# Seventh batch's one-hot rows on VectorE behind the last scores, gather tiles cleared later, its row units in other pairs, sixth batch's table as in the others

## The chip, the core and the metric

The kernel runs on one core of one Trainium2 chip. The time is device microseconds (us) of one execution; lower is better. TensorE is PE in the views (PEld its weight loads), VectorE is DVE, ScalarE is ACT, GpSimd is POOL, SyncE, which issues most transfers, is SP.

## The reference

Causal attention over 8 batches of 448 tokens (12 heads of 64) gives x (3584 x 768). A gate picks one of 8 experts for each token; each expert keeps the 80 tokens with the largest gate weights and sends them through two layers.

```python
scores = np.where(mask, -1000000000.0, scale * np.matmul(q, k.transpose(0, 1, 3, 2)))
attn = np.exp(scores - np.max(scores, axis=-1, keepdims=True))
x = np.matmul(attn / (np.sum(attn, axis=-1, keepdims=True) + 1e-09), v)   # then (N, D)
expert_idx = np.argmax(x @ w_gate, axis=1)        # gate_w: the softmax value there
for e in range(E):
    tok_idx = ...                                 # the 80 largest gate_w of expert e
    h = np.maximum(x[tok_idx] @ w1[e], 0.0)
    out[tok_idx] = gate_w[tok_idx, None] * (h @ w2[e])
```

## The kernel before

**Attention.** The program runs over 48 pairs of heads, six for each batch (batch 6 is b = 5, batch 7 b = 6, batch 8 b = 7). A pair has 8 slots. CYCLE says what stands in each: scores on PE in two parts (`s0`, `s1`, L354), the masked maximum on DVE (`m`, tile `ns`, L364), the exponential on ACT (`e`, tile `prob`, L371), the turn of the pair before in two halves on PE (`t0`, `t1`, tile `tp`, L385) with its copy on ACT (`c0`, `c1`, tile `PT`, L390), the product with v (`v`, tile `xp`, L411) and its copy on DVE (`xu`, L417). `tp` has a single buffer, so `t1` waits for the copy `c0`, and the next turn for `c1`.

**Selection.** The expert choice is a running table: every batch merges its tokens with a table of the best 80 of each expert so far. Its steps are spread over the pairs of the following batches, by tables of slot numbers that count from the end of the batch's own pairs: STEPS for most batches, NEXT for batch 6, EARLY for batch 7. What of batch 7 comes after the last pair (slot 48 on) is called in the order of TAIL, where `rest` takes the next such step, mixed with the whole selection of batch 8. The steps of importance here:

- `c3w` to `c0w`, `c3l` to `c0l`: weights compared on PE (tile `rn`), read out on DVE (`less`, L764); `rl`, `lt`: the same against the table (L782, L788); `cp`, `ro`: counts and places (L795, L800).
- `places`, `places_more`: one-hot rows `rm` of the table's entries. As a rule two DVE instructions of 80x320 (L820); where `late` is set, eight POOL instructions of 80x80 (L817).
- `gt`, `own`, `earlier`, `rank`: each token's rank; `own` is on DVE (L854, L856), `earlier` and `rank` on POOL (L849 to L859).
- `rr`: one-hot rows of the tokens (L883 on DVE, or with `late` four POOL instructions of 128x80, L879).
- `tn`: 8 products with `rm` (L893) and 4 with `rr` (L896) on PE make the new table; `tab` copies it (L907), `rp` turns it (L911), `row` copies that (L915).

**Rows of x.** They are turned on PE into two tiles `rt`, scaled into `xr` on DVE and stored to `xs` by SP: `row_tile` (L606, L617) for batches 1 to 6, `row_unit` (L576, L585) for batch 7. Its four units stand at the slots of ROWS_EARLY (head half, pair of token tiles, slot, distance of the second scaling). The tiles `rt`, `rn`, `rl`, `gp`, `tn`, `rp` and `selt` all come from `bank`, which up to the last pair has two buffers in turn (pool `ps_m`): the second tile asked for waits until the one two before it was read out.

**Batch 8** in the tail: gate products `gp` (L484), `gs` copied by ACT (L489), `lp` (L500), on DVE `lg`, `logit`, maximum, `gsh`, first pick `goh` (L512 to L661), the exponential `gex` on ACT (L648), `ggw` on DVE (L667), then the one-hot columns, their turns `selt` (L740) copied by ACT (L743), and the steps above. ACT also scales row group 2 (L547). `wp` (L1125) are products whose result nobody reads. `close` gives attention's memory free and clears the three tiles `xg` (L1113; one on DVE, two on POOL), into which the experts' rows are gathered later (L1214).

**Experts.** After batch 8's table the rows of each expert are gathered, weights are split into two halves `wh` (ACT, L1197) and `wl` (DVE, L1182), and freed weight buffers are loaded anew by SP (L200).

Of the kernel before, what the change touches and what calls it, by code (L numbers as in the profile page):

```python
# [28 lines left out]
NORMS = [0, 2, 3]  # L29
ROWS = [22, 30, 46, 54]  # L30
STEPS = {'c2w': 64, 'c1w': 72, 'cp': 72, 'gt': 80, 'tn': 88, 'rp': 92, 'row': 93, 'gp0': 16, 'gs0': 18, 'gp1': 24, 'gs1': 26, 'lp': 32, 'lg': 34, 'logit': 39, 'shifted': 40, 'chosen': 42, 'sums': 42, 'one_hot': 43, 'weight': 43, 'columns': 44, 'weighted': 44, 'parts': 45, 'r0t': 48, 'r1t': 48, 'r0c': 50, 'r1c': 50, 'c3w': 56, 'rl': 56, 'c0w': 56, 'c3l': 58, 'lt': 61, 'c0l': 63, 'c2l': 66, 'c1l': 74, 'ro': 74, 'places': 77, 'places_more': 77, 'own': 82, 'earlier': 83, 'rank': 83, 'rr': 85, 'rr_more': 85, 'tab': 90}
NEXT = {'c2w': 64, 'c1w': 72, 'cp': 72, 'gt': 80, 'tn': 86, 'rp': 88, 'row': 90, 'gp0': 16, 'gs0': 18, 'gp1': 24, 'gs1': 26, 'lp': 32, 'lg': 34, 'logit': 39, 'shifted': 40, 'chosen': 42, 'sums': 42, 'one_hot': 43, 'weight': 43, 'columns': 44, 'weighted': 44, 'parts': 45, 'r0t': 48, 'r1t': 48, 'r0c': 50, 'r1c': 50, 'c3w': 56, 'rl': 56, 'c0w': 56, 'c3l': 58, 'lt': 61, 'c0l': 58, 'c2l': 66, 'c1l': 74, 'ro': 74, 'places': 75, 'places_more': 75, 'own': 82, 'earlier': 83, 'rank': 83, 'rr': 83, 'rr_more': 83, 'tab': 87}
EARLY = {'gp0': 16, 'gs0': 18, 'gp1': 24, 'gs1': 26, 'lp': 32, 'lg': 34, 'logit': 35, 'shifted': 36, 'chosen': 38, 'sums': 38, 'one_hot': 39, 'weight': 39, 'weighted': 40, 'columns': 40, 'parts': 41, 'r0t': 45, 'r1t': 45, 'r0c': 46, 'r1c': 46, 'c3w': 48, 'rl': 49, 'c0w': 50, 'c3l': 51, 'c0l': 52, 'lt': 53, 'c2w': 54, 'c2l': 55, 'c1w': 56, 'c1l': 57, 'cp': 58, 'ro': 59, 'places': 60, 'places_more': 61, 'gt': 62, 'own': 63, 'earlier': 64, 'rank': 65, 'rr': 66, 'rr_more': 67, 'tn': 68, 'tab': 69, 'rp': 70, 'row': 71}
ROWS_EARLY = [(0, 0, 6, 1), (0, 1, 14, 1), (1, 0, 22, 4), (1, 1, 30, 4)]
LATE = 19

TAIL = """
rest3 ta ya v0 rest3 tb yb rest2 rest v1 rest2 turned vy guard invert placed rest w rest2 rest gp0 wy rest4 close piece gp1 gs
r0w r0e r1w lp rest r1e r1m rest rest r2w r2e r3w rest rest r3e lg logit shifted chosen r4w r4e r5w *2
sums one_hot wsum one_zero wmore columns r0t r0c *3 weight weighted parts hold rl r1t r1c *1 lt r3m r4m r5e r5m cp ro r6w r6e r6m  # L40
c3w c3l c2w r7w r7e r7m c2l c1w gt3 *2 c0w c1l gt2 *1 c0l *1 gt1 places *1 earlier gt0 places_more own *5 rank rr tn tab *28
"""
# [4 lines left out]
def attention_then_moe(  # L47
# [12 lines left out]
    nc = tc.nc  # L60
    B, _, NP, S = qT.shape
    N, D = out.shape
    E = wg.shape[2]
# [29 lines left out]
    def bank(shape, dtype, name):  # L93
        return (ps_x or ps_m).tile(shape, dtype, name=name, tag="x" if ps_x else "misc")
# [17 lines left out]
    NSL = (CAP + SL - 1) // SL  # L112
# [107 lines left out]
    lg = keep.tile([P, NT, H * E], F32, name="lg")  # L220
# [464 lines left out]
    def as_table(t):  # L685
        return t[:, 0:NV * E].rearrange("k (v e) -> k v e", e=E)
# [6 lines left out]
    def select_groups(bt):  # L693

        b = bt.b
        last = b == B - 1
        regular = b < B - 2 and CAP > 0
        late = b in (B - 3, B - 2)
        sm = lambda name, shape, dt=F32: spool.tile(shape, dt, name=name, tag=name, bufs=1)
        eng = nc.vector if last else nc.gpsimd  # L700

# [102 lines left out]
        def place(ro, sn, s, rm=None):  # L804

            n = min(SL, CAP - s * SL)
            halves = [(0, E // 2), (E // 2, E)]
            if rm is not None:
                halves.pop(0)
            elif NSL == 1:  # L810
                halves.pop()
            if rm is None:
                rm = spool.tile([SL, E, SL], BF16, name="rm", tag="rm", bufs=1 if NSL == 1 else 2)
            for e0, e1 in halves:
                if late:
                    for e in range(e0, e1):
                        nc.gpsimd.tensor_scalar(rm[0:sn, e, 0:n], slots_e[0:sn, s, e, 0:n], ro[0:sn, e:e + 1], None,  # L817
                                                op0=ALU.is_equal)
                    continue
                nc.vector.tensor_tensor(  # L820
                    out=rm[0:sn, e0:e1, 0:n], in0=ro[0:sn, e0:e1].unsqueeze(2).to_broadcast([sn, e1 - e0, n]),
                    in1=slots_e[0:sn, s, e0:e1, 0:n], op=ALU.is_equal)
            return rm
# [47 lines left out]
        def move(s):  # L871
            sn = min(SL, CAP - s * SL)
            got = {}

            def one_hot(t0=0, t1=NT):
                if t0 == 0:
                    got["rr"] = sm("rr", [P, NT, SL], BF16)
                for t in range(t0, t1) if late else []:
                    nc.gpsimd.tensor_scalar(got["rr"][:, t, 0:sn], slots_t[:, s, t, 0:sn], bt.rank[:, t:t + 1], None,  # L879
                                            op0=ALU.is_equal)  # L880
                if late:
                    return
                nc.vector.tensor_tensor(out=got["rr"][:, t0:t1, 0:sn],  # L883
                                        in0=bt.rank[:, t0:t1].unsqueeze(2).to_broadcast([P, t1 - t0, sn]),
                                        in1=slots_t[:, s, t0:t1, 0:sn], op=ALU.is_equal)

            def moved():
                m, moves, rr = bt.m, bt.moves, got["rr"]
                tn = got["tn"] = bank([SL, NV, E], F32, "tn")
                for i, (tab, ro, so) in enumerate(moves[:s + 1]):  # L890
                    rm = bt.places[i] if NSL == 1 else place(ro, so, s)
                    for e in range(E):
                        nc.tensor.matmul(tn[0:sn, :, e], rm[0:so, e, 0:sn], tab[0:so, :, e], start=(i == 0 and e == 0),  # L893
                                         stop=False, skip_group_check=True)
                for t in range(NT):
                    nc.tensor.matmul(tn[0:sn].rearrange("k v e -> k (v e)"), rr[:, t, 0:sn],  # L896
                                     m[:, t].rearrange("k v e -> k (v e)"), start=(t == 0 and not moves[:s + 1]),
                                     stop=(t == NT - 1), skip_group_check=True)

            def taken():  # L900
                tn, rr = got["tn"], got["rr"]
                if last:
                    finish(s, sn, tn)
                    return
                got["flat"] = tables[s][b % 2]
                tab = got["tab"] = as_table(got["flat"])
                (nc.scalar.copy if b >= B - 3 else nc.vector.tensor_copy)(tab[0:sn], tn[0:sn])  # L907

            def turn():
                rp = got["rp"] = bank([P, SL], BF16, "rp2")  # L910
                nc.tensor.transpose(rp[:, 0:sn], got["flat"][0:sn, 2 * E:2 * E + P], identb[0:sn, 0:sn])  # L911

            def row():
                row = table_rows[s][b % 2]
                (nc.scalar.copy if b >= B - 3 else nc.vector.tensor_copy)(row[0:3 * E, 0:sn], got["rp"][0:3 * E, 0:sn])  # L915
                bt.new.append((got["tab"], row))
                if s == NSL - 1:
                    table[:] = bt.new
            first, more = [one_hot], []
            if not last and NSL == 1:  # L920
                first, more = [lambda: one_hot(0, NT // 2)], [lambda: one_hot(NT // 2, NT)]
            bt.rest_of_rows = run(more)
            return first + [moved, taken] + ([] if last else [turn, row])
# [68 lines left out]
    def batch_plan(bt):  # L992
# [5 lines left out]
        if early:  # L998
            for g, half, at, x in ROWS_EARLY:
                for f, x in zip(row_unit(bt, g, half), (0, 1, x)):  # L1000
# [9 lines left out]
        if CAP:  # L1010
            steps.update(select_groups(bt))
        for name, at in (EARLY if early else NEXT if bt.b == B - 3 else STEPS).items():
            if name in steps:
# [3 lines left out]
    with tc.manual_schedule():  # L1017
# [18 lines left out]
        parts, values = [], []  # L1036
        for i, pr in enumerate(pairs):
# [22 lines left out]
            for k in range(SLOTS):  # L1060
# [9 lines left out]
                if i > 4 and k in (1, 4, 7):  # L1070
                    if not parts and len(wload) < WBUF:
                        parts = piece_parts()
# [10 lines left out]
        rest = [f for k in sorted(plan) for f in plan.pop(k)]  # L1083
# [10 lines left out]
        if CAP:  # L1094
            steps.update(select_groups(bt))
# [363 lines left out]
```

## Time and profile before

| | us |
|---|---|
| median of 3 runs | 449.97 (449.87 to 450.06) |
| the profiled execution | 450.27 |
| its span in the trace | 448.2 |
| PE, ACT, DVE, POOL busy | 421.9, 373.9, 344.8, 91.2 |
| mean granted clock of PE, share of full | 0.989 |

The profiled execution lies 0.30 us above the median, and 2.07 us of it lie outside the span. All times below are us from the start of the span. Attention's pairs end near 298, the tail with batch 8's selection runs to 326, the experts to the end.

### The profile page before, as it was taken

Reading aid. Unit: us, or ns where it says so; the run is one execution under the profiler, and the core shown is the slowest. Engines: PE = TensorE matmul, PEld = TensorE weight load, DVE = VectorE, ACT = ScalarE, POOL = GpSimd, SP = SyncE. Lnnn points to the kernel's source line nnn. Section 1 sums busy time; section 2 is a strip of 40 time slices with the busy share of each in tenths; the row PEclk is TensorE's granted clock in tenths of the full one; section 3 lists DMA queues with packets and bytes.
Section 4 is the critical chain, followed back from the end, with each engine's and each line's share of the span. In section 5 each row is a group of like instructions: output and inputs, shape, how many; then the busy total and the mean of one; then the engine's idle time right before and its main releaser. Section 6 shows DMA issues by size and latency. Waiting matters only on the chain.

```text
span 448.2 us, 18075 instructions
## 1 busy us (share of the span) xinstructions
PE 421.9 (94%) x7353; PEld 342.1 (76%) x7353; DVE 344.8 (77%) x1214; ACT 373.9 (83%) x982; POOL 91.2 (20%) x236
## 2 busy tenths in 40 slices
PE   5798999999999999999999999986998999999994
PEld 2566777777777777777777777864678999999993
DVE  4556578778978878788887887865577999999892
ACT  4999999989999898998998978872677889897891
POOL 4301002002102100300210210518440275211002
PEclk9999999999999999999999999999799999999998
DMA  8348589678884866767866352544359999999911
GB/s 307 114 148 305 186 300 318 191 279 290 258 296 173 289 238 247 252 198 272 287 208 223 116 197 89 205 145 158 106 171 341 405 400 389 392 424 424 397 40 44
DMA packets 33458, 110.07 MB, mean 246 GB/s; under 512 B 4274, under 2 KB 17074, under 8 KB 30176
## 3 DMA queue, kind: packets, MB, share of 16 engines
q1 hardware_dynamic: 32176, 105.19, 64.3%
q0 software_dynamic: 1056, 3.51, 2.5%
q8 instruction: 57, 0.93, 0.8%
q10 hardware_dynamic: 144, 0.23, 0.2%
q14 instruction: 25, 0.20, 0.1%
HBM read 85.35 MB, written 23.99 MB: 244 GB/s over the span
## 4 chain that ended last, share of the span: by engine, by line
PE 66%; ACT 16%; DVE 6%; issue 4%; DMA 4%; POOL 3%; POOLq 0%; DVEq 0%
PE sp L354 14%; PE xp L411 13%; ACT prob L371 10%; PE tp L385 9%; ACT PT L390 5%; PE op L1254 4%; PE op L1262 3%; PE hp L1269 3%; PE rt L606 3%; PE hp L1266 3%; PE hp L1268 3%; PE hp L1254 2%; DVE ns L364 2%; DMA xg<-xs,idx 2%; PE op L1264 2%
## 5 line engine op out<-in xcount | busy, mean ns | idle before, releaser
L371 ACT ACTIVATE prob<-ns,nb 128x448 f32<-128x448 f32 (+6 forms) x336 | 167.0, 500 | 26.8 <-DVE nb L364 26.5
L364 DVE CUSTOM_DVE_ANT_0 ns<-sp,mask 128x448 f32<-128x448 f32 (+6 forms) x336 | 124.0, 418 | 59.3 <-PE sp L354 35.1
L390 ACT COPY PT<-tp 128x1024 f32<-128x1024 f32 x96 | 95.9, 999 | 7.3 <-PE tp L385 7.0
L354 PE MATMUL sp<-qk 64*64 64x256 f32 (+6 forms) x1344 | 97.5, 396 | 4.5 <-DMA qk<-k_t 4.5
L411 PE MATMUL xp<-PT,vt 128*64 128x64 f32 (+3 forms) x1536 | 95.3, 277 | 0.0
L1182 DVE SCALAR_TENSOR_TENSOR wl<-wraw,wh 128x768 f16<-128x768 f32 (+1 forms) x91 | 91.8, 1065 | 3.0 <-ACT wh L1197 3.0
L411 PEld LDWEIGHTS xp<-PT,vt 128*64 128x64 f32 x1536 | 79.6, 137 | 17.6 <-issue 8.8
L1197 ACT ACTIVATE wh<-wraw 128x768 f16<-128x768 f32 (+1 forms) x91 | 78.9, 930 | 5.5 <-DMA xs<-xrl 1.7
L354 PEld LDWEIGHTS sp<-qk 64*64 64x64 f32 x1344 | 54.1, 134 | 35.8 <-issue 18.0
L385 PE MATMUL tp<-ident,prob 64*128 64x64 f32 x1536 | 68.0, 227 | 6.4 <-ACT PT L390 6.0
L385 PEld LDWEIGHTS tp<-ident,prob 64*128 64x128 f32 x1536 | 56.1, 139 | 17.0 <-ACT PT L390 8.7
L371 ACT ACTIVATION_READ_ACCUMULATOR prob<-ns,nb 128x1 f32 x336 | 63.7, 190 | 0.0
L1269 PEld LDWEIGHTS <-wl 128*128 128x128 f16 x362 | 36.1, 100 | 1.4 <-DVE wl L1182 1.4
L1268 PEld LDWEIGHTS <-wh 128*128 128x128 f16 x362 | 36.2, 100 | 0.6 <-issue 0.6
L1266 PEld LDWEIGHTS <-wh 128*128 128x128 f16 x362 | 36.4, 101 | 0.0
L417 DVE COPY xu<-xp 128x448 f32<-128x448 f32 x48 | 29.7, 619 | 8.4 <-PE xp L411 7.9
L1266 PE MATMUL hp<-xh,wh 128*128 128x80 f16 x320 | 35.3, 202 | 0.5 <-issue 0.5
L1269 PE MATMUL hp<-xh,wl 128*128 128x80 f16 x320 | 35.3, 202 | 0.0
L1268 PE MATMUL hp<-xl,wh 128*128 128x80 f16 x320 | 35.3, 202 | 0.0
L1355 POOL DMA_INDIRECT out<-yo,idx x8 | 19.7, 2466 | 65.1 <-ACT yo L1352 60.9
L1262 PE MATMUL op<-hh,wh 128*128 128x160 f16 x264 | 29.4, 233 | 0.0
L1264 PE MATMUL op<-hh,wl 128*128 128x80 f16 x264 | 28.9, 199 | 0.0
(185 smaller groups left out, 559.5 us busy)
## 6 DMA issues: line engine op xcount, KB each, us to landing
wraw<-w SPq DMA_DIRECT2D x25, 1536.0 KB, 11.2
out<-mask SPq DMA_DIRECT2D x56, 192.0 KB, 4.1
qk<-q_t SPq DMA_DIRECT2D x15, 672.0 KB, 5.1
qk<-k_t SPq DMA_DIRECT2D x15, 672.0 KB, 5.4
vt<-v_t SPq DMA_DIRECT2D x16, 576.0 KB, 7.5
wraw<-w SPq DMA_DIRECT2D x30, 256.0 KB, 5.0
xs<-xr SPq DMA_DIRECT2D x18, 384.0 KB, 4.5
wraw<-w SPq DMA_DIRECT2D x16, 192.0 KB, 4.5
```

What stands on the lines that cost most here:

```text
L354: nc.tensor.matmul(pr.sp[t][to], st["q"][rows, p, t * QB:(t + 1) * QB], st["k"][rows, p, 0:WIDTH[t]], start=True, stop=True)
L364: nc.vector.tensor_tensor_reduce(out=ns[:, 0:w], in0=pr.sp[t], in1=mask[:, S - w:S], scale=-1.0 / 8.0, scalar=HUGE, op0=ALU.add, op1=ALU.m ...
L371: nc.scalar.activation(pr.P[:, OFF[t]:OFF[t] + w], ns[:, 0:w], AF.Exp, bias=nb, scale=-1.0, accum_out=pr.sums[:, pr.p * TILES + t:pr.p * T ...
L385: nc.tensor.transpose(tp[:, r, at:at + QB], pr.P[rows, off:off + P], ident[rows, rows])
L390: (nc.scalar.copy if how == "a" else nc.vector.tensor_copy)(pr.PT[:, g], pr.tp)
L411: nc.tensor.matmul(xp[rows, x0 * QB:x1 * QB], st["vt"][:, c, p * P + j * DH:p * P + (j + 1) * DH], pr.PT[:, g, 1 - j if crossed else j, at ...
L1182: return nc.vector.scalar_tensor_tensor(out=l, in0=src, scalar=SW, in1=h, op0=ALU.mult, op1=ALU.subtract)
L1197: nc.scalar.activation(h, src, AF.Copy, scale=SW)
L1262: nc.tensor.matmul(side[i], wh[:, ws], u.both[:, c], start=(x == 0 and i % per == 0), stop=(x == n - 1), skip_group_check=True)
L1266: nc.tensor.matmul(o, wh[:, ws], ah[:, c, :], start=(x == 0 and i % per == 0), stop=False, skip_group_check=True)
L1268: nc.tensor.matmul(o, wh[:, ws], al[:, c, :], start=False, stop=False, skip_group_check=True)
L1269: nc.tensor.matmul(o, wl[:, ws], ah[:, c, :], start=False, stop=(x == n - 1), skip_group_check=True)
```

## The change

- `late` is set for batch 6 alone, so batch 7's `rm` and `rr` are DVE instructions (two of 80x320, and one of 128x320 instead of two half steps).
- `tab` and `row` run on ACT for batch 7 alone; batch 6's run on DVE.
- TAIL is in another order: `close` behind `rr` and `gp1`, `tn` ahead of `lp`, `ro` ahead of `placed`.
- ROWS_EARLY: the units stand at slots 14, 22, 30 and 46 instead of 6, 14, 22 and 30; the fourth one's second scaling falls in the tail.
- NEXT, batch 6: `tn` 86 to 88, `tab` 87 to 90, `rp` 88 to 92, `row` 90 to 93, `c3l` 58 to 61, `lt` 61 to 58, `places` 75 to 76.

```diff
-ROWS_EARLY = [(0, 0, 6, 1), (0, 1, 14, 1), (1, 0, 22, 4), (1, 1, 30, 4)]
+ROWS_EARLY = [(0, 0, 14, 1), (0, 1, 22, 4), (1, 0, 30, 4), (1, 1, 46, 8)]
...
-rest3 ta ya v0 rest3 tb yb rest2 rest v1 rest2 turned vy guard invert placed rest w rest2 rest gp0 wy rest4 close piece gp1 gs
-r0w r0e r1w lp rest r1e r1m rest rest r2w r2e r3w rest rest r3e lg logit shifted chosen r4w r4e r5w *2
+rest3 ta ya rest3 v0 tb yb rest3 rest v1 rest2 turned vy guard invert rest placed w rest2 rest gp0 wy rest5 gp1 close piece gs
+r0w r0e r1w rest lp r1e r1m rest rest r2w r2e r3w rest r3e lg logit shifted chosen r4w r4e r5w *2
...
-        late = b in (B - 3, B - 2)
+        late = b == B - 3
...
-                (nc.scalar.copy if b >= B - 3 else nc.vector.tensor_copy)(tab[0:sn], tn[0:sn])
+                (nc.scalar.copy if b == B - 2 else nc.vector.tensor_copy)(tab[0:sn], tn[0:sn])
...
-                (nc.scalar.copy if b >= B - 3 else nc.vector.tensor_copy)(row[0:3 * E, 0:sn], got["rp"][0:3 * E, 0:sn])
+                (nc.scalar.copy if b == B - 2 else nc.vector.tensor_copy)(row[0:3 * E, 0:sn], got["rp"][0:3 * E, 0:sn])
...
-            if not last and NSL == 1:
+            if b < B - 2 and NSL == 1:
                 first, more = [lambda: one_hot(0, NT // 2)], [lambda: one_hot(NT // 2, NT)]
```

On DVE in the tail, from batch 7's places to the first row group of batch 8 (`xrl`), - is before and + is now:

```order
 L431 RECIPROCAL sums<-sums 128x42
-L800 TENSOR_SCALAR rof_6693<-rn,pnum 80x8
+L800 TENSOR_SCALAR ro_6684<-rn,pnum 80x8
+L820 TENSOR_TENSOR rm<-ro_6684,slots_e 80x320 x2
 L417 COPY xu<-xp 128x448
 L854 TENSOR_TENSOR own<-gt,goh 128x32
 L856 TENSOR_REDUCE larger<-own 128x4
-L1113 MEMSET xg_6756 80x768
+L883 TENSOR_TENSOR rr<-rank,slots_t 128x320
+L1113 MEMSET xg_6752 80x768
 L553 TENSOR_TENSOR xrl<-rt,norm 128x384
```

The two `rm` rows stand ahead of the last `xu`, the `rr` row between the rank and the clearing of `xg`.

On PE in the tail, behind the first two row groups of batch 8 (`rt`), where batch 7's table is made:

```order
 L534 MATMUL rt<-ident,xu 128x128 x6
-L500 MATMUL lp<-ident,gs 128x96 x4
 L893 LDWEIGHTS rm
 L893 MATMUL tn<-tab_1_664,rm 80x5
...
 L896 LDWEIGHTS rr
 L896 MATMUL tn<-mv,rr 80x40
-L534 MATMUL rt<-ident,xu 128x128 x6
+L500 MATMUL lp<-ident,gs 128x96 x4
 L911 LDWEIGHTS tab_0_662
```

`lp` moved from ahead of the table's twelve products to behind them; two row groups moved from ahead of `rp` to behind it.

On PE at the end of the last pair (48), behind its product with v, up to the second half of its turn:

```order
 L411 MATMUL xp<-PT,vt_111 64x64 x4
+L911 LDWEIGHTS tab_1_664
+L911 MATMUL rp_6531<-identb,tab_1_664 128x80
 L740 LDWEIGHTS oh_658
...
 L740 MATMUL selt<-identb,mv 128x128
+L576 MATMUL rt_6552<-ident,xu 128x64
+L576 MATMUL rt_6553<-ident,xu 128x64
...
 L385 MATMUL tp<-ident,prob_99 128x64 x16
```

Batch 6's `rp` and batch 7's fourth row unit (twelve transposes, alternately into two tiles) now stand here; a unit at the end of pair 43, behind batch 6's last row tile, is gone.

## Rows read from the trace of the kernel before

**Rows 1.** The page's first part: busy time, share of the span and instructions

```profile
PE 421.9 (94%) x7353; PEld 342.1 (76%) x7353; DVE 344.8 (77%) x1214; ACT 373.9 (83%) x982; POOL 91.2 (20%) x236
```

**Rows 2.** Waits from 300 to 327: who waited for whom, total, times, longest

```profile
PE tn L896 <- POOL rr L879: 3.2, 4, 1.6
```

**Rows 3.** Timeline of POOL: start, length, instruction, count, idle time before it

```profile
305.10 3.72 POOL L817 TENSOR_SCALAR rm<-slots_e,rof 80x80 bf16<-80x80 f16 x8
```

**Rows 4.** Timeline of PE in the tail

```profile
307.23 0.87 PE L534 MATMUL rt<-ident,xu 128*128 128x128 f32 x6
307.96 0.55 PE L500 MATMUL lp<-ident,gs 96*128 96x96 f32 x4
...
313.03 1.52 PE L534 MATMUL rt<-ident,xu 128*128 128x128 f32 x6
...
316.61 0.61 PE L740 MATMUL selt<-identb,oh 128*128 128x128 bf16 x4
...
318.13 0.47 PE L782 MATMUL rl<-row,ex 128*128 128x80 bf16 x4
```

**Rows 5.** Windows of 1 us: PE, PEld, DVE, ACT, POOL busy, granted clock, DMA

```profile
313.00:314.00 1.00, 1.00 (x6) 1.00 (x7) 0.00 (x0) 0.19 (x1) 0.69 (x1) 0.50 0.00 0
...
319.00:320.00 1.00, 0.96 (x8) 0.58 (x7) 0.71 (x8) 0.93 (x2) 0.35 (x1) 0.96 0.28 66
```

**Rows 6.** Timeline of ACT in the tail

```profile
313.23 0.19 ACT L907 CAST tab<-tn 80x40 bf16<-80x40 f32 x1 [4.55 <-PE tn L896]
...
315.68 0.22 ACT L648 ACTIVATE gex<-gsh 128x32 f32<-128x32 f32 x1
```

**Rows 7.** Timeline of DVE in the tail

```profile
305.38 0.62 DVE L417 COPY xu<-xp 128x448 f32<-128x448 f32 x1 [1.39 <-PE xp L411]
...
306.13 0.19 DVE L856 TENSOR_REDUCE larger<-own 128x4 f32<-128x32 f32 x1
306.42 0.70 DVE L1113 MEMSET xg<- 80x768 f32 x1
...
315.93 0.19 DVE L667 TENSOR_REDUCE ggw<-gex 128x4 f32<-128x32 f32 x1 [4.92 <-ACT gex L648]
```

**Rows 8.** Lines L820 and L883: ns min/median/max, first and last start, forms

```profile
L820 DVE TENSOR_TENSOR rm<-ro,slots_e x10: 478/480/483, 132.5 to 323.2; 80x320 bf16<-80x320 f16 x10
L883 DVE TENSOR_TENSOR rr<-rank,slots_t x11: 309/310/492, 101.9 to 324.4; 128x160 bf16<-128x160 f16 x10, 128x320 bf16<-128x320 f16 x1
```

**Rows 9.** Timeline of PE in pairs 47 and 48: batch 6's table, selt, rl

```profile
289.96 0.48 PE L893 MATMUL tn<-tab,rm 80*80 80x5 bf16 x8
290.30 0.31 PE L896 MATMUL tn<-mv,rr 128*80 128x40 bf16 x4
...
296.56 0.40 PE L740 MATMUL selt<-identb,oh 128*128 128x128 bf16 x4
...
298.23 0.30 PE L782 MATMUL rl<-row,ex 128*128 128x80 bf16 x4
```

**Rows 10.** Timelines of PE and ACT at the end of pair 43

```profile
263.44 0.27 PE L576 MATMUL rt<-ident,xu 64*128 64x64 f32 x1 [0.67 <-DVE xr L617]
263.90 0.58 PE L576 MATMUL rt<-ident,xu 64*128 64x64 f32 x11 [0.19 <-DVE xr L617]
...
265.03 1.01 ACT L390 COPY PT<-tp 128x1024 f32<-128x1024 f32 x1 [1.54 <-PE tp L385]
```

**Rows 11.** Timelines of DVE, PE and ACT at the end of pair 48

```profile
297.22 0.74 DVE L743 COPY ex<-selt 24x512 bf16<-24x512 bf16 x2
...
297.11 0.71 PE L385 MATMUL tp<-ident,prob 64*128 64x64 f32 x16
...
297.86 1.01 ACT L390 COPY PT<-tp 128x1024 f32<-128x1024 f32 x1
```

**Rows 12.** Start of the experts on DVE, and the window of the experts

```profile
326.19 3.50 DVE L1182 SCALAR_TENSOR_TENSOR wl<-wraw,wh 128x1024 f16<-128x1024 f32 x3
...
330.00:440.00 110.00, 107.91 (x1978) 106.20 (x1976) 100.75 (x126) 91.87 (x151) 30.34 (x14) 1.00 0.88 344
```

More of the change, by code (lines that the diff above doesn't have):

```diff
@@ L31 @@
 STEPS = {'c2w': 64, 'c1w': 72, 'cp': 72, 'gt': 80, 'tn': 88, 'rp': 92, 'row': 93, 'gp0': 16, 'gs0': 18, 'gp1': 24, 'gs1': 26, 'lp': 32, 'lg': 34, 'logit': 39, 'shifted': 40, 'chosen': 42, 'sums': 42, 'one_hot': 43, 'weight': 43, 'columns': 44, 'weighted': 44, 'parts': 45, 'r0t': 48, 'r1t': 48, 'r0c': 50, 'r1c': 50, 'c3w': 56, 'rl': 56, 'c0w': 56, 'c3l': 58, 'lt': 61, 'c0l': 63, 'c2l': 66, 'c1l': 74, 'ro': 74, 'places': 77, 'places_more': 77, 'own': 82, 'earlier': 83, 'rank': 83, 'rr': 85, 'rr_more': 85, 'tab': 90}
-NEXT = {'c2w': 64, 'c1w': 72, 'cp': 72, 'gt': 80, 'tn': 86, 'rp': 88, 'row': 90, 'gp0': 16, 'gs0': 18, 'gp1': 24, 'gs1': 26, 'lp': 32, 'lg': 34, 'logit': 39, 'shifted': 40, 'chosen': 42, 'sums': 42, 'one_hot': 43, 'weight': 43, 'columns': 44, 'weighted': 44, 'parts': 45, 'r0t': 48, 'r1t': 48, 'r0c': 50, 'r1c': 50, 'c3w': 56, 'rl': 56, 'c0w': 56, 'c3l': 58, 'lt': 61, 'c0l': 58, 'c2l': 66, 'c1l': 74, 'ro': 74, 'places': 75, 'places_more': 75, 'own': 82, 'earlier': 83, 'rank': 83, 'rr': 83, 'rr_more': 83, 'tab': 87}
+NEXT = {'c2w': 64, 'c1w': 72, 'cp': 72, 'gt': 80, 'tn': 88, 'rp': 92, 'row': 93, 'gp0': 16, 'gs0': 18, 'gp1': 24, 'gs1': 26, 'lp': 32, 'lg': 34, 'logit': 39, 'shifted': 40, 'chosen': 42, 'sums': 42, 'one_hot': 43, 'weight': 43, 'columns': 44, 'weighted': 44, 'parts': 45, 'r0t': 48, 'r1t': 48, 'r0c': 50, 'r1c': 50, 'c3w': 56, 'rl': 56, 'c0w': 56, 'c3l': 61, 'c2l': 66, 'c1l': 74, 'ro': 74, 'places': 76, 'places_more': 76, 'own': 82, 'earlier': 83, 'rank': 83, 'rr': 83, 'rr_more': 83, 'tab': 90, 'c0l': 58, 'lt': 58}
```

## The prediction

> **What bounds the kernel now.** I read the page's busy times first. PE is at 94% of the span, ACT at 83%, DVE at 77%, POOL at 20% [rows 1]: as an average, nothing that moves work off POOL should matter. But the average mixes three stages. In attention PE hardly rests; in the experts it is busy for 107.91 of 110 us while the transfers take 0.88 of theirs [rows 12]; between them lies the tail, where one chain runs through all engines in turn and every wait on it is time. So I read the waits of the tail. The largest one of PE is for POOL: the four products with `rr` wait 3.2 us in all [rows 2]. POOL's list shows why: its eight `rm` instructions take 3.72 us from 305.10, and the rank and `rr` are queued behind them [rows 3].
>
> Two more things hang on that wait. The windows show the granted clock at 0.50 (the 1.2 GHz level) at 313, right behind it, and back at 0.96 in the window from 319 [rows 5]. And ACT gets to batch 7's `tab` only at 313.23, with `gex` of batch 8 behind it in its list, so that DVE, which had batch 8's logits ready, sits idle for 4.92 us until 315.93 [rows 6, 7]. That idle time is the best measure of what the wait costs: DVE was ready at 315.93 - 4.92 = 311.01.
>
> In attention I looked at the two places where a row unit comes or goes. At the end of pair 43 two groups of turns stand one behind the other, the second waits for DVE to read out the first's tiles (0.67 and 0.19 us), and ACT is idle for 1.54 us before it can copy the next half turn [rows 10]. At the end of pair 48 there is none of this: ACT begins that copy at 297.86, right as PE's turn (0.71 us from 297.11) is done [rows 11].
>
> **The change part by part.**
>
> *Batch 7's rows on DVE.* The two `rm` instructions take 0.48 us each and `rr` 0.49 [rows 8]. The two `rm` lie in front of the last `xu`, where DVE is idle for 1.39 us [rows 7]: 0.96 us fits, nothing is late. Without that gap they would cost 0.96. `rr` needs `larger`, done at 306.13 + 0.19 = 306.32 [rows 7], then one small POOL addition, and is wanted by PE when its six row turns are over, at 307.96 (where `lp` began) [rows 4]. That leaves 1.64 us for the addition and the 0.49: no wait on PE is left there. The gather tiles' clearing (0.70 us on DVE [rows 7]) follows `rr` and is covered, since DVE then waits for `lp`; uncovered it would cost these 0.70. On POOL it now stands behind the rank instead of between two parts of `rr`.
>
> *`tn` ahead of `lp`.* In pair 47, where nothing was missing, the table's twelve products took from 289.96 to 290.30 + 0.31 = 290.61, so 0.65 us [rows 9]. Batch 8's `lp` thus starts 0.65 later, and DVE has its logits ready at 311.01 + 0.65 = 311.66. ACT must not be later: from `tab` to the end of `gex` it took 315.68 + 0.22 - 313.23 = 2.67 us [rows 6], with PE at half clock. `tab` can now run at about 307.96 + 0.65 + 0.1 = 308.7, which puts `gex` at 311.4. So DVE's logits are what ends last, and `ggw` moves from 315.93 to 311.66: **-4.27 us**. Bounds: -3.2, if only PE's own wait comes back [rows 2], and -4.92, if `lp` costs nothing.
>
> *The clock.* Between `ggw` and the next comparison two groups of four `selt` turns and the four `rl` products lie on the chain. At half clock they took 0.61 and 0.47 us, in attention 0.40 and 0.30 [rows 4, 9]: 2 x 0.21 + 0.17 = 0.59. I take **-0.6 us**, with 0 as the other end. The level fell behind a stretch in which PE had almost nothing; what is left now, from the last row turns to `selt`, is about 1 us. The Trainium skill's page "TensorE: Matmul & The Clock Gate" (Part 1: The HAM clock gate) says that the half rate is the default and that activity lifts it; by that, too, the full rate should stay, and the trace agrees with its 0.50 and 0.96.
>
> *The unit gone from pair 43.* PE is spared the waits of 0.67 and 0.19 and twelve transposes of 0.58, together 1.44; ACT could start 1.54 earlier [rows 10]. I take **-1.5 us**. The other end is 0, if another engine holds that pair.
>
> *The unit added to pair 48.* `bank` has two buffers there, and the asking order is `rp`, `selt`, and the unit's two tiles: the second one needs the buffer of `selt`, which DVE frees with its copies `ex`, done at 297.22 + 0.74 = 297.96 [rows 11]. Behind that instruction on PE stand eleven more transposes and the half turn `t1`; ACT's copy waits for it, and the tail's first turn for ACT. So 297.96 + 0.58 + 0.71 = 299.25 instead of 297.86 [rows 10, 11]: 1.4, less some overlap, **+1.3 us**. Ends: 0.3, if DVE gets to `ex` a microsecond sooner, and 1.4. The unit's two scalings on DVE lie where it waits for PE in the tail. Its two stores on SP stand ahead of the last weight piece loaded in the tail, which nobody needs before the experts at 326 [rows 12]. The other three units only change places.
>
> *Batch 6.* `tab` and `row` leave ACT, which in pair 48 is the fuller engine; about 0.2 us each by the row of batch 7's [rows 6]. Part of it shows: **-0.1 us** (0 to -0.4). `tn` goes from one side of a turn to the other, and `lt` and `c3l` change places in the same pair: no term.
>
> *Sum.* -4.27 - 0.6 - 1.5 + 1.3 - 0.1 = -5.17 us. From `ggw` on, batch 8's chain is the same row for row, and the experts begin with it, `wl` right behind its last places at 326.19 [rows 12], so the whole last stage moves along. The profiled execution took 450.27, which gives 445.10; the median lies 0.30 below it: **444.8 us**.
>
> **The rivals.** What a measurement of this kernel can tell from no change is about 0.2%, 0.9 us.
>
> 1. *Another wait takes POOL's place.* If `gex` or the logits come later than I worked out and the half clock stays, only 3.2 of 4.87 us come back: 444.8 + 1.7 = 446.5. For it speaks that DVE and ACT are within 0.3 us of each other at `ggw`, and that PE still has a short rest before `selt`.
>
> 2. *Pair 43 gives nothing.* If ACT or DVE holds that pair, the 1.5 is lost and pair 48's 1.3 stays: 446.3. Against it: ACT is idle for all of 1.54 there.
>
> 3. *The last stage does not move.* If the experts' start hung on transfers, the gain would be waited away there: about 450. Against it: `wl` begins as soon as batch 8's places are there.
>
> 4. *The busier engine takes the work (slower).* POOL is the emptiest engine and DVE is at 77%. If DVE were what limits the tail, its 2 x 0.48 + 0.49 = 1.45 us more would be added and nothing come back: 449.97 - 0.3 + 1.45 = 451.1. It decides as soon as DVE has no idle time left in front of `xu` and `ggw`; it has 1.39 and 4.92 us [rows 7]. The Trainium skill's page "Perfetto Trace Analysis" (Identifying the Most-Contended Engine) says to find the engine of the highest occupancy and to optimize that one first; taken over the whole span it speaks for this rival, while the same page's advice to look at each regime by itself speaks against it, as do the rows.
>
> 5. *The clock falls in pair 48 already (slower).* PE now rests there until 297.96 for the unit's tile. If the half rate came there and stayed through the tail, its steps would grow as the six row turns did, 1.52 against 0.87 [rows 4], by three quarters: the stretch from 297.96 to 307.96 is 10 us, some 8.5 of it on PE, so +6.4: 451.2. It decides from about 5 us on. Against it: at pair 43 PE rested in two pieces as well, and the execution's mean granted clock of 0.989 leaves hardly more room for the half rate than the tail's 6 us of it take.
>
> **How the numbers follow.** The forecast 0.64, its own range 443.9 to 445.8; rival 1 0.15, rival 2 0.09, rival 3 0.05, rivals 4 and 5 0.07 together. All good ends together (-4.92, -0.6, -1.5, +0.3, -0.4) would be 442.9, all bad ends (-3.2, 0, 0, +1.4, 0) 448.2; no single case needs either. The range goes from 443.6 to rivals 1 and 2 and a little beyond, 447.0, which leaves out about one in eight. Faster by over 0.2%: 0.64 + 0.15 + 0.09 = 0.88; within: 0.05; slower: 0.07.
>
> **What the profile of the changed kernel would show.** PE has no wait for POOL at `tn`, and DVE's `rr` ends before PE's row turns. `ggw` stands some 4 us earlier against the end of attention, with little idle time before it. The granted clock is 1.00 through the tail, and six row turns behind `rp` take 0.87 again. At the end of pair 43 ACT's gap before its copy is down to some tenths; at the end of pair 48 the unit's second transpose waits for `ex` and ACT has a new gap of about 1.3. The experts' window is as long as before. I am wrong if `ggw` is again preceded by several us of idle DVE, or if the experts take longer.

## The result, and the profile after

The changed kernel took 444.36 us (median of 7 executions, 442.08 to 447.08), the kernel before 449.94 on the same chip: ratio 0.989, 95% interval 0.985 to 0.992. The forecast was 444.8 (443.6 to 447.0). The profiled execution of the changed kernel was its quickest, 442.08 us with a span of 440.1. Both kernels' profiled executions, stretch by stretch (us; a pair holds two of ACT's copies `PT`, and the stretches of attention run between every second one):

| stretch | before | after | difference | forecast |
|---|---|---|---|---|
| start, until ACT's copy before the end of pair 43 | 257.34 | 257.07 | -0.27 | none |
| the end of pair 43 (to the next such copy) | 7.69 | 6.04 | -1.65 | -1.5 |
| to the end of pair 47 | 26.78 | 26.50 | -0.28 | -0.1 |
| the end of pair 48 | 6.05 | 7.38 | +1.33 | +1.3 |
| to the last `xu` on DVE | 7.52 | 7.52 | 0 | 0 |
| last `xu` to `ggw` | 10.55 | 6.04 | -4.51 | -4.27 |
| `ggw` to the first `wl` | 10.26 | 9.34 | -0.92 | -0.6 |
| first `wl` to the end | 122.0 | 120.2 | -1.8 | 0 |

The five forecast terms came to -6.0 instead of -5.17, and two things were in no term of the sum: the last row, and a loss of the clock in pair 48 that this execution does not show and others do (below).

PE's list of waits of the changed kernel (us in total, times, longest): the 3.2 us for POOL of [rows 2] are gone. The two longest waits for DVE are the one ahead of `selt` and a new one in pair 48 (`rt` for `ex`).

```profile
PE tp L385 <- ACT PT L390: 6.9, 11, 1.5
...
PE selt L740 <- DVE oh L706: 1.3, 1, 1.3
PE rt L576 <- DVE ex L743: 0.9, 1, 0.9
```

PE in the tail of the changed kernel, against [rows 4]: `tn` comes right behind the six row turns, `lp` begins 0.46 us after it, and the row turns behind them take 1.51 for twelve where six took 1.52.

```profile
306.37 0.87 PE L534 MATMUL rt<-ident,xu 128*128 128x128 f32 x6
307.08 0.45 PE L893 MATMUL tn<-tab,rm 80*80 80x5 bf16 x8
307.38 0.31 PE L896 MATMUL tn<-mv,rr 128*80 128x40 bf16 x4
307.54 0.53 PE L500 MATMUL lp<-ident,gs 96*128 96x96 f32 x4
...
308.01 1.51 PE L534 MATMUL rt<-ident,xu 128*128 128x128 f32 x12
...
311.23 0.40 PE L740 MATMUL selt<-identb,oh 128*128 128x128 bf16 x4 [1.34 <-DVE oh L706]
```

DVE, POOL and ACT there, against [rows 3, 6, 7]: `rm` lies ahead of the last `xu`, whose wait falls from 1.39 to 0.46; `rr` waits only 0.38 us, for POOL's short addition; behind `lg` DVE now runs through to `ggw` with no idle time. `gex` on ACT (310.30, 0.22 us long) was over 0.03 us before `ggw` began, so the two engines are almost level. The four copies of `norm` on POOL took 1.36 us beside DVE's `rm`.

```profile
303.15 0.90 DVE L820 TENSOR_TENSOR rm<-ro,slots_e 80x320 bf16<-80x320 f16 x2
...
304.51 0.63 DVE L417 COPY xu<-xp 128x448 f32<-128x448 f32 x1 [0.46 <-PE xp L411]
...
305.83 0.49 DVE L883 TENSOR_TENSOR rr<-rank,slots_t 128x320 bf16<-128x320 f16 x1 [0.38 <-POOL rank L859]
...
308.17 0.61 DVE L512 TENSOR_TENSOR lg<-lp,norm 128x288 f32<-128x288 f32 x2 [0.59 <-PE lp L500]
...
310.55 0.19 DVE L667 TENSOR_REDUCE ggw<-gex 128x4 f32<-128x32 f32 x1
...
303.21 1.36 POOL L450 COPY norm<-sums 64x12 f32<-64x12 f32 x4 [10.82 <-DVE ro L800]
...
305.60 0.20 POOL L859 TENSOR_TENSOR rank<-rank,larger 128x4 f16<-128x4 f16 x1 [0.47 <-DVE larger L856]
305.73 1.41 POOL L1113 MEMSET xg<- 80x768 f32 x2
...
307.73 0.19 ACT L907 CAST tab<-tn 80x40 bf16<-80x40 f32 x1
...
310.30 0.22 ACT L648 ACTIVATE gex<-gsh 128x32 f32<-128x32 f32 x1
```

Windows of the changed kernel (busy us of PE, PEld, DVE, ACT, POOL, then granted clock, DMA share, GB/s): the clock is full at 313, where [rows 5] had 0.50, and also in the window in which PE rests.

```profile
310.00:311.00 1.00, 0.00 (x0) 0.00 (x0) 0.78 (x7) 0.88 (x4) 0.00 (x0) 1.00 0.29 103
...
313.00:314.00 1.00, 0.94 (x8) 0.66 (x8) 0.71 (x7) 0.82 (x2) 1.00 (x3) 1.00 0.00 0
```

ACT's copy at the end of pair 43 has no idle time ahead of it ([rows 10] had 1.54). At the end of pair 48 the added unit's turns wait for `ex`, and ACT for them ([rows 11] had neither):

```profile
263.11 1.00 ACT L390 COPY PT<-tp 128x1024 f32<-128x1024 f32 x1
...
295.90 0.55 PE L576 MATMUL rt<-ident,xu 64*128 64x64 f32 x11 [0.91 <-DVE ex L743]
...
296.99 1.01 ACT L390 COPY PT<-tp 128x1024 f32<-128x1024 f32 x1 [1.46 <-PE tp L385]
```

### The profile page after: what moved, and what is told of

Same layout as the page of the kernel before. It is cut to its first block, busy times and chain, and to the rows that moved or that the text cites. A ratio compares the mean times of both kernels' runs of the same rounds, so it can differ in the third digit from the quotient of the medians.

```text
span 440.1 us, 18062 instructions
## 1 busy us (share of the span) xinstructions
PE 417.2 (95%) x7353; PEld 339.2 (77%) x7353; DVE 346.3 (79%) x1219; ACT 373.3 (85%) x980; POOL 85.7 (19%) x224
```

## The experiments

Theory: each term does in the profile what the prediction said, the wait for POOL above all; the spread of the executions and the shorter experts have a cause of their own. Rivals stand with each run. Ratios are to the kernel before on the same chip, with their 95% interval.

### The tail alone

```diff
-late = b in (B - 3, B - 2)
+late = b == B - 3                      # and TAIL as changed, rr in one step
...                                     # ROWS_EARLY, NEXT, engine of tab and row: as before
```

> Batch 7's rows on DVE, tn ahead of lp and the later clearing alone; the row units, batch 6's table and its order as in the kernel before. If the wait for POOL carries the gain (my theory): the tail gives -4.5 us to ggw and -0.8 by the clock as in the changed kernel, and -0.3 of batch 6's changes is missing, so about 444.7 us against 449.9, ratio 0.988 (0.987 to 0.990), and ggw follows the last xu by about 6.0 us (10.55 in the kernel before). Rival, the row units carry part of the tail's gain by setting DVE free: ggw comes back by 3.2 us only and the time is 446.5 or more. If the experts' 1.8 us also come with the tail, 443.

445.45 us, ratio 0.988 (0.985 to 0.991). The last `xu` to `ggw` took 6.05 us, `ggw` to the first `wl` 9.34: -4.51 and -0.92, all of the tail's gain. The experts took 122.6, so their 1.8 us do not come with the tail.

### The row units alone

```diff
-ROWS_EARLY = [(0, 0, 6, 1), (0, 1, 14, 1), (1, 0, 22, 4), (1, 1, 30, 4)]
+ROWS_EARLY = [(0, 0, 14, 1), (0, 1, 22, 4), (1, 0, 30, 4), (1, 1, 46, 8)]
...                                     # all else as in the kernel before
```

> The row units in the other pairs alone, all else as in the kernel before. My theory: the end of pair 43 gives -1.65 us and the end of pair 48 takes +1.33, so 449.6 us, ratio 0.9993 (0.998 to 1.000), with ACT's first copy at the end of pair 43 some 1.6 us earlier against pair 42 and the one at the end of pair 48 1.3 later against pair 47. Rival, pair 43's gain is hidden or comes from batch 6's order: 451.2 us, ratio 1.003. Rival, the unit in pair 48 stalls only because DVE has batch 6's table too: no loss there, 448.3.

450.42 us, ratio 0.998 (0.996 to 1.001): no difference that can be told. The steps show how the two changes cancel: ACT's copy at the end of pair 43 came 1.62 us earlier against the one before it, that at the end of pair 48 1.33 later. (This execution had lost 1.27 us at the start, with the granted clock at 0.96 in the first 40 us.)

### The fourth unit in pair 47

```diff
-ROWS_EARLY = [... (1, 1, 46, 8)]
+ROWS_EARLY = [... (1, 1, 38, 4)]        # in the changed kernel
```

> The changed kernel with the fourth row unit in pair 47, where nobody asks for selt before it, in place of pair 48. My theory: the wait for ex goes and the 1.3 us come back, 443.0 us against the changed kernel's 444.4, ratio to before 0.986. Rival, the work costs as much wherever it stands (12 transposes, two tiles of PSUM, two scalings): the new wait shows at the end of pair 47 and the time stays at 444.4, ratio 0.989.

443.71 us, ratio 0.983 (0.980 to 0.987), between what I expected (443.0) and the rival's 444.4. From ACT's copy before the end of pair 43 to the last `xu` it took 46.29 us instead of 47.44: 1.15 of the 1.33 came back. The missing 0.18 lies at the end of pair 48 (6.22 us where the kernel before has 6.05). The new place has a wait of its own, of PE for `xr`; that it makes the 0.18 is not shown.

```profile
290.71 0.44 PE L893 MATMUL tn<-tab,rm 80*80 80x5 bf16 x8 [0.70 <-DVE xr L585]
```

### More filling products ahead of selt, and the changed kernel again

```diff
-... r3e lg logit shifted chosen r4w r4e r5w *2
+... r3e lg logit shifted chosen r4w r4e r5w *6
```

> The changed kernel with six instead of two filling products in PE's rest of 1.3 us ahead of selt. My theory: that executions of the changed kernel lie between 442.1 and 447.1, with a mean granted clock of 0.990 in the longest, comes of the clock falling in that rest in some of them; with the rest filled no run is over 445 and the median is 442 to 443.5. Rival, the spread has another origin: runs up to 447 again, median 444.4. Rival, the four products come too late and push selt back: up to +0.5 us on every run.

> The changed kernel once more, unaltered, for its other executions. Two of its seven were 447.1 long at a mean clock of 0.990, and the profiled one, 442.08, had the experts 1.8 us shorter than the kernel before. My theory: the usual execution has the experts at about 122 us with PE's wait of about 1 us for the second gather, as in all other kernels so far, and lasts about 444.3; one that loses the clock in pair 48 lasts 446 to 447; one without the gather's wait 442. Rival, the experts are shorter in most executions because the changed kernel starts them on freer queues: median 442 to 443.

With the rest filled the kernel took 443.35 us, ratio 0.983 (0.979 to 0.987). The median lies where I had put it, but two executions took 446.0 and 446.3, so my theory, that the rest ahead of `selt` makes the long executions, fell. The unaltered kernel took 445.19, ratio 0.989 (0.986 to 0.991), and the rival of shorter experts in most executions (442 to 443) fell too. Both profiled executions showed the loss elsewhere. PE and windows of the changed kernel's second profile, in pair 48:

```profile
295.83 0.55 PE L576 MATMUL rt<-ident,xu 64*128 64x64 f32 x11 [0.91 <-DVE ex L743]
...
297.99 1.12 PE L385 MATMUL tp<-ident,prob 64*128 64x64 f32 x16 [0.58 <-ACT PT L390]
299.04 2.66 PE L411 MATMUL xp<-PT,vt 128*64 128x128 f32 x20
...
298.00:299.00 1.00, 1.00 (x16) 0.92 (x16) 1.00 (x10) 0.00 (x0) 0.00 (x0) 0.50 0.09 37
299.00:300.00 1.00, 1.00 (x11) 0.77 (x10) 0.63 (x3) 0.80 (x1) 0.00 (x0) 0.50 0.00 0
```

Behind the waits of 0.91 and 0.58 us the clock stood at its half level (1.2 GHz) for some 3 us, and from ACT's copy before the end of pair 43 to the last `xu` it took 48.97 us instead of 47.44. Three of the six profiles with the unit in pair 48 (the filled one and the one with `lp` first are the others) show this loss of 1.5 us, none of the eight without it, the kernel before among them. The first profile has the same two waits and kept the full clock, so the waits alone do not decide it.

### Unit in pair 47 and filled

```diff
-ROWS_EARLY = [... (1, 1, 46, 8)]
+ROWS_EARLY = [... (1, 1, 38, 4)]
...
-... r3e lg logit shifted chosen r4w r4e r5w *2
+... r3e lg logit shifted chosen r4w r4e r5w *6
```

> The changed kernel with the fourth row unit in pair 47 and with six filling products ahead of selt. In the run with the filling products alone the profiled execution showed the clock at half level from 298.4 to 301.5, behind the wait for the unit's tile in pair 48, and lost 1.66 us there. If that fall makes the long executions, here none is over 444.5, no mean clock is under 0.995 and the median is 442.5 to 443.5. Rival, the clock falls in other places too: runs of 0.992 and about 444.8 again, median as with the unit moved alone (443.7).

442.16 us, ratio 0.983 (0.980 to 0.987), but the long executions of the rival came, so there is more than one kind: 440.97, 441.16 and 441.21 beside 443.11, 444.69 and 444.92. Pair 48's clock is not all of the spread. So I set the profiles' experts side by side. They took 120.2 to 120.4 us in three (the changed kernel's first, this one, and the next), and 121.9 to 122.6 in the other seven so far. The changed kernel's first profile, with the gathers on POOL, the first `wl`, the first weight load and the second `xtp`:

```profile
319.93 1.08 POOL L1214 DMA_INDIRECT xg<-xs,idx  x1 [3.47 <-DVE gws L965]
321.32 1.84 POOL L1214 DMA_INDIRECT xg<-xs,idx  x1 [0.31 <-issue]
...
319.89 3.57 DVE L1182 SCALAR_TENSOR_TENSOR wl<-wraw,wh 128x1024 f16<-128x1024 f32 x3
...
323.49 23.54 SPq L200 DMA_DIRECT2D wraw<-w  x7
...
330.45 0.58 PE L1232 MATMUL xtp<-ident,xg 80*128 80x80 f32 x6
```

And its second profile, in which the second `xtp` waits:

```profile
321.59 1.95 POOL L1214 DMA_INDIRECT xg<-xs,idx  x1 [3.65 <-DVE gws L965]
323.84 1.85 POOL L1214 DMA_INDIRECT xg<-xs,idx  x1 [0.31 <-issue]
...
321.36 3.50 DVE L1182 SCALAR_TENSOR_TENSOR wl<-wraw,wh 128x1024 f16<-128x1024 f32 x3
...
324.89 20.55 SPq L200 DMA_DIRECT2D wraw<-w  x6
...
333.02 0.61 PE L1232 MATMUL xtp<-ident,xg 80*128 80x80 f32 x6 [0.93 <-DMA xg<-xs,idx]
```

The first gather waits for `idx` and for the last row store to land; in all twelve profiles whose trace has that landing, it begins 1.0 us after it. Begun with DVE's first `wl` or before it, its instruction takes 1.08 us; begun 0.2 us later, it takes 1.95. The second gather's is then over only at 325.69, behind the start of the weight load at 324.89, and PE waits 0.93 us for its data; in the first profile it was over at 323.16, ahead of the load at 323.49. The load begins 4.2 to 4.3 us after `idx` in both, as the third `wl` ends. The kernel before has the long order already:

```profile
328.68 1.85 POOL L1214 DMA_INDIRECT xg<-xs,idx  x1 [0.31 <-issue]
...
329.72 18.42 SPq L200 DMA_DIRECT2D wraw<-w  x5
...
337.83 0.61 PE L1232 MATMUL xtp<-ident,xg 80*128 80x80 f32 x6 [0.92 <-DMA xg<-xs,idx]
```

### The clock alone

```diff
-r0w r0e r1w lp rest r1e r1m
+r0w r0e r1w lp *12 rest r1e r1m        # in the kernel before
```

> The kernel before with twelve filling products on PE (some 3.2 us) between lp and the products with rr, where PE waits for POOL; nothing is taken off POOL. It prices the clock alone. If my second term is right, the wait for POOL and the 4.9 us of DVE ahead of ggw stay, the granted clock is 1.00 through the tail, the stretch from ggw to the first wl shrinks from 10.26 us to about 9.35 as in the changed kernel, and the time is 0.9 us under the kernel before, ratio 0.998. Rival, most of the changed kernel's gain in the tail is the clock's: 2 us or more, ratio under 0.996. Rival, the clock falls all the same: ratio 1.000.

447.41 us, ratio 0.993 (0.991 to 0.995): more than I expected, on the rival's side. The rows divide it. The windows from 312 to 320 all stand at 1.00; the last `xu` to `ggw` shrank by 0.43, `ggw` to the first `wl` by 0.61, to 9.65, and not to the 9.35 that I had put on the clock. That is 1.0 us of clock; DVE still waits 4.53 ahead of `ggw`. The other 1.6 us are the experts, 120.4: the first gather's instruction took 1.08 us and PE had no wait for the second, in this profile and, by their narrow spread (447.24 to 447.64), presumably in all six executions.

```profile
315.45 0.19 DVE L667 TENSOR_REDUCE ggw<-gex 128x4 f32<-128x32 f32 x1 [4.53 <-ACT gex L648]
```

### lp ahead of tn

```diff
-r0w r0e r1w rest lp r1e r1m ...
+r0w r0e r1w lp rest r1e r1m ...
```

> The changed kernel with lp ahead of tn again in the tail, as in the kernel before. The prediction priced tn ahead of lp at 0.65 us. If lp is on the path, ggw follows the last xu by 5.4 us instead of 6.04 and the time is 0.65 under the changed kernel's. Rival, ACT's row copies and tab, which then come later, hold gex: ggw follows by 6.0 to 6.6 us, and the time is the same or up to 0.6 longer.

446.55 us, ratio 0.991 (0.988 to 0.994). The last `xu` to `ggw` took 6.46 us, 0.41 more: ACT's list, with `tab` and the row copies later, holds `gex`. The rival was right: against this order `tn` ahead of `lp` has no price, but gains 0.4.

```profile
312.68 0.19 DVE L667 TENSOR_REDUCE ggw<-gex 128x4 f32<-128x32 f32 x1 [0.89 <-ACT gex L648]
```

### rr on POOL again

```diff
+late_rr = b in (B - 3, B - 2)          # rr on POOL, rm on DVE; TAIL as in the changed kernel
```

> The changed kernel with rr of batch 7 on POOL again, as four instructions of about 0.47 us, rm staying on DVE. If the eight rm ahead of rank and rr are what blocked the tail (3.72 of POOL's 6 us), POOL has rr done at 307.7 on the changed kernel's scale, PE waits at most 0.4 us and ggw follows the last xu by 6.0 to 6.5 us: the time is 0 to 0.4 us over the changed kernel's, 444.7. Rival, any POOL work between larger and tn costs the whole wait: ggw follows by 7.5 us or more, and the time is 446 or over.

445.47 us, ratio 0.991 (0.987 to 0.994). PE's longest wait for `rr` was 0.17 us and the last `xu` to `ggw` took 6.40. So `rr` on POOL costs 0.35, and the block was what stood ahead of its parts.

```profile
306.03 1.87 POOL L880 TENSOR_SCALAR rr<-slots_t,rankf 128x80 bf16<-128x80 f16 x4
...
307.96 0.21 PE L897 MATMUL tn<-mv,rr 128*80 128x40 bf16 x1 [0.17 <-POOL rr L880]
```

That was not the eight `rm` (3.72 us, [rows 3]) alone. In the kernel before the clearing of two `xg` tiles stands between the halves of `rr`, and PE's longest wait lies behind it:

```profile
309.63 0.97 POOL L879 TENSOR_SCALAR rr<-slots_t,rankf 128x80 bf16<-128x80 f16 x2
310.56 1.41 POOL L1113 MEMSET xg<- 80x768 f32 x2
311.94 0.94 POOL L879 TENSOR_SCALAR rr<-slots_t,rankf 128x80 bf16<-128x80 f16 x2
...
312.48 0.26 PE L896 MATMUL tn<-mv,rr 128*80 128x40 bf16 x1 [1.61 <-POOL rr L879]
```

The clearing put `rr`'s end back by some 1.4 us, the `rm` by the rest. Here, as in the changed kernel, both are out of the way; no run moves one of them alone, so how the 4.5 us divide stays an estimate: some 1.4 for the clearing and 3 for the `rm`.

### The race ahead of the experts, from three sides

```diff
-ROW_ENGINES = "vpappppp"
+ROW_ENGINES = "vpappppv"               # last row group (r7) on DVE; unit in pair 47, *6
```

> The kernel with the unit in pair 47 and six filling products, and besides the last row group of batch 8 scaled by DVE instead of ACT and POOL. In all profiles so far the first gather's instruction on POOL took 1.08 us where it began before or with DVE's first wl and 1.2 to 1.95, until 2.85 after idx began, where it began later; in the first case idx to the second xtp took 11.2 us, in the second 12.3 to 12.6 with PE waiting about 1 us for the second gather, and the experts were 2 us longer. If the race between the landing of the last row store (which the gather waits for) and DVE's first wl makes the difference, the store now lands some 0.8 us earlier, every execution is of the first kind, at a price of up to 0.5 us on DVE's chain: executions of 441.7, up to 443 where the clock falls in the start-up, none near 444.8. Rival, the spread is the transfers' own: half of the executions at 443.5 or more.

441.42 us, ratio 0.981 (0.978 to 0.984), the quickest here: five executions from 441.03 to 441.93, one of 443.27. The first gather's instruction took 1.08 us, the experts 120.2; `ggw` to the first `wl` paid 0.47 for it.

```diff
+for i in range(3):                     # ahead of gws and wl; unit in pair 47, *6
+    nc.vector.tensor_reduce(fill[:, i:i + 1], mask[:, 0:256], axis=AX.X, op=ALU.add)
```

> The same race from the other side: the kernel with the unit in pair 47 and six filling products, and three reductions on DVE (together about 1.1 us, their result unused) ahead of the first wl, whose delay is covered by the 2.15 us that DVE sits idle ahead of xl. If the race decides, the first gather begins ahead of wl in each execution, its instruction takes 1.08 us, idx to the second xtp takes 11.2 us, and the executions lie at 441.2 (442.6 where the clock falls in the start-up), median 441.3. Rival, wl's own start or the weight load behind it is what the experts wait for: 1.1 us more in every execution, 442.3 and 445.9.

444.09 us, ratio 0.986 (0.983 to 0.989): a miss. The first gather did get in, 1.08 us, but the second then met the delayed `wl`, took 3.57 us to 323.54, 0.8 behind the start of the weight load at 322.74, and PE waited 1.68 us; behind that wait the granted clock stood at 0.50 from 332 to 335, so not all of the 123.1 us of experts is the wait. Its POOL and DVE rows:

```profile
319.97 3.57 POOL L1217 DMA_INDIRECT xg<-xs,idx  x1 [0.31 <-issue]
...
320.36 2.35 DVE L1185 SCALAR_TENSOR_TENSOR wl<-wraw,wh 128x1024 f16<-128x1024 f32 x2
```

So it is not the first gather's own delay that counts. What all long cases share is a weight load that starts before POOL is done issuing the second gather. The last run moves only that:

```diff
-load_piece()
+if not marks:
+    marks.append(nc.sync.dma_start(mark, highs[7][0:1, 0:1]))   # two bytes; waits for the 8th wh
+with tc.issue_after(marks[0].ins):     # unit in pair 47
+    load_piece()
```

> The kernel with the unit in pair 47 alone, and a two-byte transfer on SP's queue ahead of the experts' first weight load, which waits for ACT's eighth wh. In every profile with long experts (nine of thirteen) that load began at 4.2 us after idx, 0.8 us before POOL was done issuing the second gather, and PE waited 0.5 to 1.7 us for that gather; in the four with short experts it began 0.3 us after. Here it can begin only some 4.9 to 5.6 us after idx, behind the second gather's issue, whether POOL was held up by DVE or not. If the order of load and gather is what costs the 2 us, PE's wait for the second gather goes and the executions lie at 441.0 to 441.9, up to 443.2 where the clock falls in the start-up. Rival, POOL's hold-up itself, by which both gathers come 1 us later, is the cost: PE waits 0.5 us or more as with the unit moved alone, median 443.7.

442.49 us, ratio 0.983 (0.980 to 0.985), the ratio of the run with the unit in pair 47 alone, and only one of the six executions within the 441.0 to 441.9 that I had set. The rows say more. The first gather was held up, 1.39 us, as in the long cases; the load began at 324.40, behind the second gather's end at 323.19, and PE did not wait:

```profile
319.64 1.39 POOL L1219 DMA_INDIRECT xg<-xs,idx  x1 [4.21 <-DVE gws L965]
321.34 1.85 POOL L1219 DMA_INDIRECT xg<-xs,idx  x1 [0.31 <-issue]
...
324.40 14.66 SPq L200 DMA_DIRECT2D wraw<-w  x5
...
329.42 0.58 PE L1237 MATMUL xtp<-ident,xg 80*128 80x80 f32 x6
```

The experts took 121.1 us. Five of the six spans lie at 439.7 to 440.2 (with the unit in pair 47 alone they run from 439.0 to 443.3); the time outside the span was 1.7 to 3.1 us here, which blurs the total. So the order of load and gather makes PE's wait. What is left, 0.7 to 0.9 us over the short experts, is the hold-up together with a load that began 6.2 us after `idx` instead of 4.2; this run does not part the two.

## Why the prediction was right, and where it was not

**The wait for POOL** was the right thing to read: -4.51 measured, -4.27 forecast. The milestone (DVE's readiness at 311.01) was right, and the 0.65 added for `tn` was the mis-sized part: `lp` began only 0.46 us behind `tn`'s begin, since it did not wait for the end of the last product (0.15 later), and `ggw` came 0.41 behind the milestone. The run with `lp` first shows that the good end, -4.92, could not be had that way, since ACT would then have ended last. That `gex` and the logits stand within 0.3 us of each other, as rival 1 noted, is what the profile after shows; its wait did not come. Part of the 4.51 is the clock's: with the clock alone, 0.43 of it came back.

**The clock between `ggw` and the experts**, forecast -0.6, gave -0.61 in the run with the clock alone. The stretch shrank by 0.92, and the other 0.31 is not the clock's: the run with `rr` on POOL has a granted clock of 1.00 all through it and takes 9.66 us as well. The prediction took batch 8's chain to be the same row for row. It is not: in the kernel before, as in the runs with `rr` of batch 7 on POOL, DVE carries one more semaphore instruction ahead of each of `lt`, `less`, `larger` and `rr`, which the runs with `rr` on DVE do not have, and their idle times there add up to the 0.3. Why they are needed no run here shows. The one ahead of `rr` in the kernel before:

```profile
L883 DVEq EVENT_SEMAPHORE  x1: 21/21/21, 324.4 to 324.4; - x1
```

**The units** gave -1.65 and +1.33 for -1.5 and +1.3; the run with the units alone confirms both steps, and that they cancel within what its time can tell.

**Batch 6's part** gave nothing where I had put it: pair 48 takes 7.38 us with the units alone, where `tab` and `row` are still on ACT, and 7.38 in the changed kernel. The -0.28 lies in pair 44 (6.74 us before, 6.45 after; 6.65 with the units alone), where `lt` and `c3l` changed places and where I had put no term. That the measured -0.28 lies within the 0 to -0.4 given for it is luck.

**Rival 5 happened in small.** I priced the clock's fall in pair 48 as lasting through the tail, +6.4 us. Where it falls, it is back after some 3 us and costs about 1.5. The argument against it, that pair 43 has two rests as well, did not hold: it falls in three of the six profiles that have the unit there. The profiled execution of a kernel cannot show this for a kernel that does not have the rest yet.

**The experts' stage as long as before** was right for most executions, as their spans tell, and wrong for the profiled one. The assumption hid a race that the kernel before already has: its row store lands 0.5 us after `idx` begins, and its second gather is overtaken by the weight load, with PE's wait of 0.92.

With the usual 122 us of experts the changed kernel's span is 448.2 - 6.3 = 441.9 us, or 443.4 with pair 48's loss; with the 2.0 outside it, 443.9 to 445.4. Nine of its thirteen executions lie at 443.8 to 445.8. Five of the thirteen have a mean granted clock of 0.989 to 0.994 (spans 443.6 to 445.1; the profile with the loss has 0.994), the other eight 0.995 or more (spans 440.1 to 442.8). The median of 444.36 is one of the eight, so it holds neither the short experts nor pair 48's loss. It agrees with the forecast to 0.4 us partly by luck: the terms and the start gave 1.1 us more than I had summed, and 0.7 of that does not show in the median; 0.2 of it can be the experts (122.2 in the second profile), the rest is open. The three executions of 447.1, with 0.989 and 0.990, would need another 1.3 us or so, the size of the clock's loss at the start in the run with the units alone; no trace of the changed kernel shows that, and it stays argued.

Rivals 2, 3 and 4 fell: pair 43 gave its gain, the experts moved along, and DVE took the work in idle time.

## What to carry to other kernels

Where an engine's list stands ahead of a join, count everything that is queued in front of the wanted instruction: eight `rm` ahead of `rr` and a clearing between its halves cost 4.5 us here, `rr` itself on the same engine 0.4. Before a buffer is asked for by a new user, see who still holds it, since the wait costs its own length and, in some executions, the clock behind it. When executions spread, lay several profiles side by side at one milestone: here the order of two transfers, decided by 0.2 us, made about 2 us.

## What the runs showed of the hardware that I had not expected

POOL's gather instruction is longer beside DVE's `wl`. The first gather's took 1.08 us where it began with the first `wl` or ahead of it, and 1.2 to 1.95 where it began 0.2 to 1 us into it, then always ending 2.84 us after `idx` began. The second gather's took 3.57 in one case, ending 0.83 after the third `wl`. The Trainium skill's page "SBUF — State Buffer" (SBUF: two separate sides) says that DVE and GpSimd share one port pair by an exclusive lock, and that a transfer issued by GpSimd looks blocked because GpSimd cannot write its descriptors while DVE runs an instruction in a mode that takes both ports. These rows agree with it in kind; whether `wl` runs in such a mode no run here shows.

The four copies of `norm` on POOL took 0.91 us in the kernel before and 1.36 to 1.38 in every profile in which DVE's two `rm` run beside them. The same section of the Trainium skill's page says that a DVE instruction with two SBUF inputs locks out a GpSimd one that reads SBUF; `rm` has two inputs and `norm` reads `sums`, so these rows agree.

The granted clock fell behind rests of 0.91 and 0.58 us in pair 48 in three of six profiles, and did not fall in the tail of the changed kernel, where PE rests 1.34 us in one piece.
